# Activation sums for two groups in one instruction, the last group's casts inside an output projection, and one load on ScalarE's queue

## The chip, the cores and the metric

The kernel runs on one core of one Trainium2 chip. A core has a matrix engine (TensorE, "PE" in the profile; its weight loads are "PEld"), three engines for elementwise work (VectorE "DVE", ScalarE "ACT", GpSimd "POOL"), and a sync engine (SyncE, "SP") that here only issues transfers. Each engine has its own instruction queue, which it works off in order; ScalarE's queue can issue transfers as well. The metric is the device time of one execution in microseconds (us). Times in the trace are us from the start of the span.

## What is computed

Block-wise linear attention with a decay for each head (batch 4, 8 heads, 768 positions, head size 64) gives x with 3072 rows of 512; a gated feed-forward block with a hidden size of 1536 follows.

```python
intra = np.einsum('bhic,bhjc->bhij', qb, kb) * Dmask[None]
intra = np.einsum('bhij,bhjd->bhid', intra, vb)
inter = np.einsum('bhid,bhde->bhie', qb * lam_pow[None], kv_state)
out[:, :, sl] = intra + inter
kv_state = lam_block[None, :, None, None] * kv_state + np.einsum('bhsd,bhse->bhde', kb_dec, vb)
...
g = x @ w_gate
silu = g * (1.0 / (1.0 + np.exp(-g)))
val = x @ w_val
return (silu * val @ w_out).astype(np.float32)
```

## The kernel before

**Tiles and groups.** The 3072 rows are six tiles t = 0..5 of 512 rows; each tile is two groups of 256 rows, so there are twelve groups g = 0..11, and tile t needs groups 2t and 2t+1. For a group: k, q and v are loaded (`load_group`, line 263: for the later groups four transfers of 128 KB for k, four for q, two of 256 KB for v, all on SP's queue, L122); k is cast by ScalarE and q is scaled by VectorE (`cast_scaled`, L278 and L280), then one transposing transfer on SP turns both (L271); v is scaled by GpSimd (`v_scale`, L258). `attend(g)` (line 858) issues the inter products of group g (L498), the state update of group g+1 (L404, copied out by ScalarE at L426), the scores of group g+1 (L372, masked by VectorE at L377), the intra products of group g (L511), and two ScalarE copies into the activations `xt` (L523). GpSimd's `state` (L459) adds up states; for groups 8 to 10 ScalarE copies them to bf16 (L439, L441) some steps later, out of a list that `kv_flush` empties.

**Feed-forward, tiles 0 to 3.** A step (`ffn_fc`) takes 128 of the 1536 hidden columns: four gate matmuls (L554) into one PSUM bank, Silu on ScalarE (L558), four value matmuls (L570) into another bank, and VectorE's product of the two into `h` (L573). There are eight banks, used in turn, so a matmul waits until the bank that it writes has been read. Tiles 2 and 3 have twelve steps each; `plan` lists by hand what else is issued after a step's matmuls.

**Sums and differences.** The output projections from tile 1 on (`out_units`), and the hidden layer of tiles 4 and 5 (`ffn_unit`), use seven block products in place of eight. They need sums of operands, all on VectorE: of `wo` (L619), of `h` (`h_combo`, L636), of the weights (`w_combo`, L662) and of the activations (`x_combo`, L679). One call of `x_combo(t, n, g)` is one of four sums for one group of tile t, an instruction over 128x256 elements. So a tile takes eight; sums are read by `ffn_unit` of that tile alone.

**The order around the change.** VectorE's order is written out by hand in two ways. Work in `plan` follows a given step. Work in the list `trickle` is issued from its head, a few at a time (`drip`): one or two after each step whose plan holds no attend, cast or v_scale, and between the products of `out_units`, whose argument `many` (M2 for tile 2, M3 for tile 3) says how many follow each pair of products, and at three places of `ffn_unit` (D0, D1, D2).

In the twelve steps of tile 3 (steps 0 to 11, lines 1109 to 1139): cast of group 10 and load of group 11 after step 6; w_combo after steps 8 and 9; `attend(9)` after step 10; the sums of tile 4's first group after step 8 (line 1139, XC = 8); the cast of group 11 after step 11 (line 1135, C11 = 11). Then: `out_units(2)` (line 1169), seven pairs of products p1, p7, p6, p2, p5, p4, p3, with the second group's sums of tile 4 at the head of `trickle` (line 1168); `ffn_unit(4, 0)`, which holds the scores of group 11 (`early`) and the inter products of group 10; `ffn_unit(4, 1)` with tile 5's first-group sums ahead in `trickle` (line 1193); `out_units(3)` with the second group's (line 1197); `ffn_unit(4, 2)`; and tile 5.

The sums of tile 4 take a buffer of the pool that also holds the transposed q and k (`qkt`, three buffers); those of tile 5 one of the ten `raw` buffers that the loads of k and q use.

Of the kernel before, what the change touches and what calls it, by code (L numbers as in the profile page):

```python
# [19 lines left out]
@with_exitstack  # L20
def kernel(
    ctx: ExitStack,
    tc: tile.TileContext,
    q: bass.AP,
    k: bass.AP,
    v: bass.AP,
    lam: bass.AP,
    moe_w_gate: bass.AP,
    moe_w_val: bass.AP,
    moe_w_out: bass.AP,  # L30
    out: bass.AP,
):
    nc = tc.nc
    with tc.manual_schedule():
        _body(ctx, tc, nc, q, k, v, lam, moe_w_gate, moe_w_val, moe_w_out, out)


def _body(ctx, tc, nc, q, k, v, lam, moe_w_gate, moe_w_val, moe_w_out, out):
# [62 lines left out]
    def gsrc(t, g, h0):  # L101
        b, i = groups[g]
        return bass.AP(tensor=t.tensor,
                       offset=t.offset + b * H * S * D + i * 2 * BLK * D + h0 * S * D,
                       ap=[[2 * D, 2 * M], [S * D, H - h0], [1, 2 * D]])
# [3 lines left out]
    def load_fp32(g, eng, src, what, h0=0, h1=H):  # L109
        if (what, g) not in st:  # L110
            st[(what, g)] = (v_pool if what == "v" else raw_pool).tile(
                [128, H, 2 * D], FP32, name=what, tag="v" if what == "v" else "raw")
        t = st[(what, g)]
        if g < NAT0:
            eng.dma_start(out=t[:, h0:h1], in_=gsrc(src, g, h0)[:, 0:h1 - h0])  # L115
            return
        b, i = groups[g]
        base = src.offset + b * H * S * D + i * 2 * BLK * D
        parts = [(0, 128, False)] if what == "v" else [(0, M, False), (M, M, True)]
        for s in range(2):  # L120
            for p0, n, rev in parts:
                eng.dma_start(  # L122
                    out=t[p0:p0 + n, :, s * D:s * D + D],
                    in_=bass.AP(tensor=src.tensor,
                                offset=base + (H - 1) * S * D * rev + (p0 + s * BLK) * D,
                                ap=[[D, n], [-S * D if rev else S * D, H], [1, D]]))
# [82 lines left out]
    def qfac(g):  # L209
        return bap(dec, [[8, H], [1, 2], [0, D]], 2) if g < NAT0 else bap(qdn, [[2, H], [1, 2], [0, D]])  # L210
# [52 lines left out]
    def load_group(g, parts="kqv"):  # L263
        for src, what in ((k, "kraw"), (q, "qraw"), (v, "v")):
            if what[0] in parts:
                load_fp32(g, nc.sync, src, what)

    def dma_transpose(g):
        t = st[("qk", g)]
        tt = qkt_pool.tile([128, 2, 2, HP, 128], BF16, name="qkt", tag="qkt")  # L270
        nc.sync.dma_start(out=tt.rearrange("p a s h n -> p (a s h) n"),  # L271
                          in_=t.rearrange("p a s x -> p (a s x)"), transpose=True)
        st[("qkt", g)] = tt

    def cast_scaled(g, eng=nc.vector):
        t = qk_pool.tile([128, 2, 2, H * D], BF16, name="qk", tag="qk")
        st[("qk", g)] = t
        nc.scalar.copy(out=t[:, 0].rearrange("p s (h d) -> p h s d", h=H),  # L278
                       in_=st[("kraw", g)].rearrange("p h (s d) -> p h s d", s=2))
        eng.tensor_tensor(out=t[:, 1].rearrange("p s (h d) -> p h s d", h=H),  # L280
                                in0=st[("qraw", g)].rearrange("p h (s d) -> p h s d", s=2),
                                in1=qfac(g), op=ALU.mult)
        dma_transpose(g)
# [35 lines left out]
                        op=ALU.mult)  # L319


    later = []

    def run_later(n):
# [123 lines left out]
    def state(g):  # L448
        b, i = groups[g]
        last = i == NG // B - 1  # L450
        us = st[("ups", g)]
        f = None if i == 0 else kvs[b]
        kv = st.setdefault(("kv", g), [kv0[b][i % 2]])
        for n, u in enumerate(us):
            if f is None:
                f = u
            else:
                o = kv_pool.tile([128, HP, D], FP32, name="kvf", tag="kvf", bufs=4)
                nc.gpsimd.tensor_tensor(out=o, in0=f, in1=u, op=ALU.add)  # L459
                f = o  # L460
            if n == (3 if g >= NAT0 else 1):
                nc.gpsimd.tensor_tensor(out=kvs[b], in0=f, in1=bap(lamgrp, [[1, HP], [0, D]]), op=ALU.mult)
                nc.gpsimd.tensor_copy(out=kv0[b][(i + 1) % 2], in_=kvs[b])
            elif len(kv) == n + 1:
                o = kv_pool.tile([128, HP, D], BF16, name="kvn", tag=f"kvn{n}", bufs=2)
                kv.append(o)
                if g in KVA:
                    kvq.append((len(kvq_now), lambda g=g, n=n, o=o, f=f: kv_copy(g, n, o, f, nc.scalar.copy)))
                else:
                    kv_copy(g, n, o, f, nc.gpsimd.tensor_copy)  # L470
# [47 lines left out]
    def evac(g, fns=(nc.scalar.copy, nc.scalar.copy)):  # L518
        op, xt = st[("op", g)], st[("xt", g // 2)]
        for r in range(2):  # L520
            if fns[r] is None:
                continue
            fns[r](out=xt[:, g % 2, :, r].rearrange("p h (m s) -> p h s m", s=2) if g < NAT0 else  # L523
                   xt[:, g % 2, :, :, r * M:r * M + M],
                   in_=op[r].rearrange("p (h s m) -> p h s m", h=HP, s=2))
# [112 lines left out]
    trickle = []  # L638

    def drip(n):  # L640
        for _ in range(min(n, len(trickle))):
            trickle.pop(0)[1]()
# [25 lines left out]
    def x_combo(t, n, g):  # L668


        xt = st[("xt", t)]
        b11, b12 = xt[:, g, 0:KH, 0], xt[:, g, 0:KH, 1]
        b21, b22 = xt[:, g, KH:MC, 0], xt[:, g, KH:MC, 1]
        if t not in xs:
            pool, tag = (qkt_pool, "qkt") if t == XS0 else (raw_pool, "raw")
            xs[t] = pool.tile([128, 3, 2, KH, BLK], BF16, name="xs", tag=tag)
        x = [xs[t][:, m, g] for m in range(3)]
        o, i0, i1 = ((x[0], b12, b11), (x[1], b22, x[0]), (x[2], b21, x[1]), (b12, b22, b12))[n]
        nc.vector.tensor_tensor(out=o, in0=i0, in1=i1, op=ALU.subtract)  # L679
# [318 lines left out]
    def step(t, fc, b0=0, b1=B):  # L998
        steps.append((t, fc, b0, b1))
        return len(steps) - 1  # L1000

    def at(n, fn, *a):
        plan.setdefault(n, []).append((fn, a))
# [3 lines left out]
    at(s0[2], w_cast)  # L1007
    at(s0[2], w_piece, 8, 10)
    at(s0[3], load_group, 2, "kq")
    at(s0[3], w_piece, 10, 12)  # L1010
    at(s0[3], swapped_q_table)
    at(s0[4], w_cast)
    at(s0[4], state, 1)
    at(s0[4], load_fp32, 2, nc.sync, v, "v", 0, H // 2)
    at(s0[4], load_fp32, 2, nc.sync, v, "v", H // 2, H)
    at(s0[5], load_group, 3)
    at(s0[6], w_cast)
    at(s0[7], load_group, 4, "kq")
    at(s0[7], cast_half, 2, 0, (ACTC, POOLC))
    at(s0[7], cast_half, 2, 1, (ACTC, POOLC))  # L1020
# [6 lines left out]
    at(s0[9], run_later, 4)  # L1027
    at(s0["11a"], upd_core, 2, SPLIT)
    at(s0[10], cast_scaled, 3, nc.gpsimd)
    at(s0[10], load_group, 4, "v")  # L1030
    at(s0["11b"], v_scale, 3, nc.gpsimd)
# [4 lines left out]
    s1a = [step(1, fc, 0, 2) for fc in range(FC)]  # L1036
    s1b = [step(1, fc, 2, 4) for fc in range(FC)]
    at(s1a[3], cast_scaled, 4)
    at(s1a[3], load_group, 5, "v")
    for c in range(0, FC, 2):  # L1040
# [54 lines left out]
    XC = 8  # L1095
    D0 = (0, 0, 3)
    D1 = (0, 0, 3)
    D5 = 0
# [4 lines left out]
    KM = 2  # L1103
    A8 = 5
    A9 = 10
    C11 = 11
    sns = {0: s1a, 1: s1b + s2h}
    AT = {2: (7, 10), 3: (A8, A9)}
    for t in range(2, 4):
        order = [c for j in range(FC // 4) for c in (2 * j, 2 * j + 1, FH + 2 * j, FH + 2 * j + 1)]  # L1110
        sn = [step(t, fc, 2 if t == 2 and fc < NH else 0) for fc in (range(FC) if t == 2 else order)]
# [20 lines left out]
            at(sn[7], h_combo, t, (0, 2))  # L1132
        at(sn[11], h_combo, t, 2)
    sn = sns[3]
    at(sn[C11], cast_scaled, 11)
    for x, n, i, j0, j1 in WS:
        at(sns[x // 100][x % 100], w_combo, i, n, (j0, j1))
    for n in (0, 3, 1, 2):
        at(sn[XC], x_combo, 4, n, 0)

    for n, (t, fc, b0, b1) in enumerate(steps):
        if t >= 1 and t + 1 < NG // 2 and ("xt", t + 1) not in st:
# [19 lines left out]
    def soon(fn, *a):  # L1162
        return 0, lambda: fn(*a)

    def x_soon(t, g):
        return [soon(x_combo, t, n, g) for n in (0, 3, 1, 2)]

    trickle[:0] = x_soon(4, 1)
    out_units(2, many=list(M2))
    for c in range(2):  # L1170
        v_scale(11, nc.gpsimd, c * H // 2, (c + 1) * H // 2)
# [5 lines left out]
    def mid(g):  # L1177
        fixed[:] = [s0, s1]
        core_a(g)
# [10 lines left out]
    upd_copy(11)  # L1190
    intra(10, False)
    state(11)
    trickle[D5:D5] = x_soon(5, 0)
    ffn_unit(4, 1, (aG, aV, eG, eV, bG, bV), lambda: evac(10), lambda: mid(11), D1)
    core_b(11)
    drip(sum(x[0] <= 3 for x in trickle))
    trickle[:0] = x_soon(5, 1)
    out_units(3, bk=(aG, eG, bG, aV, eV, bV), many=list(M3))
    aG, aV, eG, eV, bG, bV, s0, s1 = aG, aV, bG, bV, s0, s1, eG, eV
    ffn_unit(4, 2, (aG, aV, eG, eV, bG, bV), dr=D2)  # L1200
# [41 lines left out]
```

## Time and profile before

| what | value |
|---|---|
| runs of the kernel, median of 3 (lowest to highest) | 221.33 us (220.85 to 221.67) |
| the profiled execution | 221.05 us |
| its span, first to last instruction | 218.9 us |
| TensorE busy, share of the span | 210.0 us, 96% |
| VectorE | 150.8 us, 69% |
| ScalarE | 129.8 us, 59% |
| GpSimd | 93.5 us, 43% |
| mean granted clock of TensorE | 0.997 |

The span leaves out what lies ahead of the first and behind the last instruction, 2.15 us here. An engine's busy time counts its compute instructions only; issuing a transfer and waiting for a semaphore aren't in it. In a timeline a line has the start, the length, the engine and source line, the operation with its output and inputs, how many were merged, and in brackets how long the engine stood idle ahead of it and whose end released it. "SPq" and "ACTq" stand for work of a queue itself, such as issuing a transfer. The chain of waits is the work that ended last, followed back from the last instruction.

### The profile page before, as it was taken

The numbers are of one execution on the slowest core, as the hardware profiler recorded it, in microseconds if no ns is written. First come the engines' busy times: TensorE is split into PE (matmuls) and PEld (weight loads), VectorE is DVE, ScalarE is ACT, GpSimd is POOL, SyncE is SP. The second block draws the span as 40 slices with busy tenths as digits, with TensorE's granted clock in tenths as the row PEclk, the third lists the DMA queues.
The fourth block names the chain that finished last, engine by engine and source line by source line (L and its number), as shares of the span: only waits on it lengthen the run. The fifth ranks groups of instructions, "written<-read, shape, count | busy, mean of one in ns | idle before, by whom it ended". The sixth has DMA issues, their size and how long they took to land.

```text
span 218.9 us, 6889 instructions
## 1 busy us (share of the span) xinstructions
PE 210.0 (96%) x2816; PEld 153.1 (70%) x2816; DVE 150.8 (69%) x275; ACT 129.8 (59%) x280; POOL 93.5 (43%) x126
## 2 busy tenths in 40 slices
PE   8889989999999999999999997999999999999993
PEld 4666435888888447766654544888788888888882
DVE  1764336576687989866387979796798479961750
ACT  6788567656636154638376677655882766636522
POOL 6675645727598150776854236130650022200200
PEclk9999999999999999999999999999999999999998
DMA  6999999999997977989679859782000400004014
GB/s 188 345 350 333 376 339 302 294 238 234 314 366 146 205 209 179 245 200 252 154 175 256 182 128 209 166 202 85 4 4 3 192 0 3 0 3 192 0 51 145
DMA packets 88321, 39.77 MB, mean 182 GB/s; under 512 B 57698, under 2 KB 83938, under 8 KB 88290
## 3 DMA queue, kind: packets, MB, share of 16 engines
q1 hardware_dynamic: 87090, 38.74, 65.5%
q10 hardware_dynamic: 1200, 0.59, 0.9%
q8 instruction: 22, 0.36, 0.7%
q14 instruction: 9, 0.07, 0.1%
HBM read 28.31 MB, written 6.29 MB: 158 GB/s over the span
## 4 chain that ended last, share of the span: by engine, by line
PE 78%; DMA 8%; SPq 6%; DVE 2%; ACT 1%; issue 1%; POOL 1%; POOLq 1%; DVEq 0%
PE bank L788 21%; PE bank L570 16%; PE bank L554 16%; PE bank L698 15%; PE bank L589 5%; DMA qraw<-in_q_dram 4%; DMA wraw<-in_moe_w_val_dram 3%; SPq L115 3%; SPq L233 3%; PE bank L511 2%; PE bank L498 2%; PE bank L404 1%; PE bank L346 1%; ACT sil L725 1%; PE bank L372 1%
## 5 line engine op out<-in xcount | busy, mean ns | idle before, releaser
L573 DVE TENSOR_TENSOR h<-sil,bank 128x256 bf16<-128x256 bf16 (+1 forms) x67 | 34.9, 532 | 27.1 <-PE bank L570 17.3
L570 PE MATMUL bank<-xt,wv_sb 128*128 128x256 bf16 (+1 forms) x268 | 52.4, 319 | 0.7 <-DVE h L573 0.7
L554 PE MATMUL bank<-xt,wg_sb 128*128 128x256 bf16 (+1 forms) x268 | 52.5, 319 | 0.0
L558 ACT ACTIVATE sil<-bank 128x256 bf16<-128x256 f32 (+1 forms) x67 | 31.8, 479 | 23.2 <-PE bank L554 18.5
L570 PEld LDWEIGHTS <-wv_sb 128*128 128x128 bf16 x268 | 26.1, 98 | 16.5 <-issue 1.0
L258 POOL TENSOR_TENSOR v_s<-v,dec 128x512 bf16<-128x512 f32 (+1 forms) x18 | 24.3, 1364 | 25.1 <-DMA v<-in_v_dram 16.5
L554 PEld LDWEIGHTS <-wg_sb 128*128 128x128 bf16 x268 | 25.2, 98 | 13.7 <-DVE xt L523 0.2
L728 POOL TENSOR_TENSOR h<-sil,es 128x512 bf16<-128x512 bf16 x6 | 7.0, 1163 | 49.3 <-ACT sil L725 49.3
L788 PEld LDWEIGHTS <-h 128*128 128x128 bf16 x240 | 23.3, 98 | 3.5 <-issue 0.3
L788 PE MATMUL bank<-wo_sb,h 128*128 128x256 bf16 x180 | 21.6, 273 | 0.1
L788 PEld LDWEIGHTS <-hs 128*128 128x128 bf16 x180 | 17.6, 98 | 2.9
L353 DVE TENSOR_TENSOR ssb<-bank,causal 128x512 bf16<-128x512 f32 x24 | 15.4, 682 | 1.8 <-PE bank L346 1.8
L698 PEld LDWEIGHTS <-ws 128*128 128x128 bf16 x144 | 13.8, 97 | 2.4 <-issue 0.2
L459 POOL TENSOR_TENSOR kvf<-kvs,ups 128x256 f32<-128x256 f32 x8 | 6.7, 839 | 19.8 <-ACT ups L426 19.8
L740 DVE TENSOR_TENSOR bank<-bank,es 128x512 f32<-128x512 f32 x12 | 7.8, 693 | 10.5 <-PE bank L698 9.0
L788 PE MATMUL bank<-wt,hs 128*128 128x256 bf16 x120 | 15.0, 272 | 0.0
L725 ACT ACTIVATE sil<-bank 128x512 bf16<-128x512 f32 x18 | 10.7, 594 | 6.9 <-POOL h L728 4.6
L728 DVE TENSOR_TENSOR h<-sil,bank 128x512 bf16<-128x512 bf16 x18 | 12.3, 683 | 1.5 <-ACT sil L725 1.4
L523 ACT CAST xt<-bank 128x512 bf16<-128x512 f32 x19 | 11.6, 655 | 2.4 <-PE bank L511 1.9
L698 PE MATMUL bank<-xs,ws 128*128 128x256 bf16 x96 | 13.0, 272 | 0.0
L459 POOL TENSOR_TENSOR kvf<-kvf,ups 128x256 f32<-128x256 f32 x16 | 12.6, 785 | 0.9
L698 PE MATMUL bank<-xt,wg_sb 128*128 128x256 bf16 x72 | 10.8, 273 | 0.2 <-ACT ups L426 0.2
(119 smaller groups left out, 362.9 us busy)
## 6 DMA issues: line engine op xcount, KB each, us to landing
out_dram<-osb SPq DMA_DIRECT2D x22, 256.0 KB, 2.1
v<-in_v_dram SPq DMA_DIRECT2D x18, 256.0 KB, 4.6
woraw<-in_moe_w_out_dram SPq DMA_DIRECT2D x6, 512.0 KB, 7.3
kraw<-in_k_dram SPq DMA_DIRECT2D x24, 128.0 KB, 3.2
qraw<-in_q_dram SPq DMA_DIRECT2D x24, 128.0 KB, 3.3
wraw<-in_moe_w_gate_dram SPq DMA_DIRECT2D x5, 512.0 KB, 7.7
wraw<-in_moe_w_val_dram SPq DMA_DIRECT2D x5, 512.0 KB, 6.6
kraw<-in_k_dram SPq DMA_DIRECT2D x4, 512.0 KB, 6.6
```

Source lines behind the costliest of these rows:

```text
L258: eng.tensor_tensor(out=st[("vs", g)][:, h0:h1], in0=st[("v", g)][:, h0:h1].rearrange("p h (s d) -> p h s d", s=2), in1=vfac(g, h0, h1), o ...
L353: nc.vector.tensor_tensor(out=ssb[:, h2, 2 * c:2 * c + 2].rearrange("p a s n -> p a (s n)"), in0=sp[(c, h2)].rearrange("p (a x) -> p a x", ...
L459: nc.gpsimd.tensor_tensor(out=o, in0=f, in1=u, op=ALU.add)
L523: fns[r](out=xt[:, g % 2, :, r].rearrange("p h (m s) -> p h s m", s=2) if g < NAT0 else xt[:, g % 2, :, :, r * M:r * M + M], in_=op[r].rea ...
L554: nc.tensor.matmul(gp[:, 0:N], wg_sb[:, mc, fs], xt[:, b0 // 2:b1 // 2, mc].rearrange("p g b n -> p g (b n)"), start=(mc == 0), stop=(mc = ...
L558: nc.scalar.activation(sil[:, 0:N], gp[:, 0:N], AF.Silu)
L570: nc.tensor.matmul(vp[:, 0:N], wv_sb[:, mc, fs], xt[:, b0 // 2:b1 // 2, mc].rearrange("p g b n -> p g (b n)"), start=(mc == 0), stop=(mc = ...
L573: nc.vector.tensor_tensor(out=h_sb[:, fc % FH, b0:b1].rearrange("p b n -> p (b n)"), in0=sil[:, 0:N], in1=vp[:, 0:N], op=ALU.mult)
L698: nc.tensor.matmul(o[:, fi * 256:fi * 256 + 256], lhs(i, c, 2 * j + fi), rhs(c), start=(start and fi == 0 and c == 0), stop=(c == KH - 1), ...
L725: nc.scalar.activation(sil[key], src, AF.Silu)
L728: eng.tensor_tensor(out=h_of(half, r), in0=v3(sil[half, r]), in1=v3(src), op=ALU.mult)
L788: nc.tensor.matmul(o, lhs(f), rhs(f), start=(start and f == 0), stop=(f == FH - 1), skip_group_check=True)
```

## The change

1. `x_combo` takes None for the group: one instruction then covers both groups (128x512 elements). Tiles 4 and 5 use it (XM = (1, 1)): four sums each, not eight. The four of tile 4 after step 8 of tile 3 and the four of tile 5 ahead of `ffn_unit(4, 1)` are gone; the joined sums are issued inside `out_units(2)` and `out_units(3)`.
2. The cast of group 11 (ScalarE copy, VectorE product, transposing transfer on SP) goes from the plan of step 11 into `trickle`: its order in `out_units(2)` is "cxwh", the cast, the four sums, nothing for w (W3L is empty), then what was in the list. With M2 beginning 1, 1, 0, 2, 1 the cast follows p1, the first sum p7, two sums p2, the last p5. Step 11's plan then has no cast, so it drips.
3. The four transfers of k of group 11 are issued by ScalarE's queue (KACT), behind the cast of group 10 and ahead of step 7's Silu; those of q and v stay on SP's.

QP is empty, so the line in `cast_scaled` changes nothing.

```diff
     def load_group(g, parts="kqv"):
         for src, what in ((k, "kraw"), (q, "qraw"), (v, "v")):
             if what[0] in parts:
-                load_fp32(g, nc.sync, src, what)
+                load_fp32(g, nc.scalar if what == "kraw" and g in KACT else nc.sync, src, what)
...
+    QP = ()
+
     def cast_scaled(g, eng=nc.vector):
+        eng = nc.gpsimd if g in QP else eng
...
+    KACT = (11,)
...
         xt = st[("xt", t)]
+        g = slice(0, 2) if g is None else slice(g, g + 1)
         b11, b12 = xt[:, g, 0:KH, 0], xt[:, g, 0:KH, 1]
...
-    C11 = 11
+    C11 = None
...
-    at(sn[C11], cast_scaled, 11)
+    if C11 is not None:
+        at(sn[C11], cast_scaled, 11)
+    XM = (1, 1)
+    W3L = ()
+    TR2 = "cxwh"
...
-    for n in (0, 3, 1, 2):
-        at(sn[XC], x_combo, 4, n, 0)
+    if not XM[0]:
+        for n in (0, 3, 1, 2):
+            at(sn[XC], x_combo, 4, n, 0)
...
-    trickle[:0] = x_soon(4, 1)
+    xw = dict(x=x_soon(4, None if XM[0] else 1),
+              c=[soon(cast_scaled, 11)] if C11 is None else [],
+              w=[soon(w_combo, i, 3, (j, j + 1)) for j in W3L for i in range(2)], h=trickle[:])
+    trickle[:] = [y for z in TR2 for y in xw[z]]
+    trickle += [] if "h" in TR2 else xw["h"]
+    trickle += [] if "c" in TR2 else xw["c"]
     out_units(2, many=list(M2))
...
-    trickle[D5:D5] = x_soon(5, 0)
+    trickle[D5:D5] = [] if XM[1] else x_soon(5, 0)
     ffn_unit(4, 1, (aG, aV, eG, eV, bG, bV), lambda: evac(10), lambda: mid(11), D1)
     core_b(11)
     drip(sum(x[0] <= 3 for x in trickle))
-    trickle[:0] = x_soon(5, 1)
+    trickle[:0] = x_soon(5, None if XM[1] else 1)
     out_units(3, bk=(aG, eG, bG, aV, eV, bV), many=list(M3))
```

## The prediction

> **What bounds the kernel now.** I read the page's chain of waits first, then the chain in order of time, then the engines' timelines around its non-TensorE pieces, then where transfers land. All times are us from the span's start; the span is 218.9.
>
> The chain by line, from the page:
>
> ```profile
> PE 78%; DMA 8%; SPq 6%; DVE 2%; ACT 1%; issue 1%; POOL 1%; POOLq 1%; DVEq 0%
> ```
>
> The DMA and SPq shares lie in the first 31.7 us, which the change doesn't touch. From there on the end is set by TensorE, so an edit is worth what it takes from, or adds to, TensorE's idle time. The chain in order of time (start, length, what) leaves TensorE only a few times in the half that is touched; the first place is this:
>
> ```profile
> 133.16 0.42 PE bank L498 x32
> 133.64 0.56 issue
> 134.21 0.42 DVE h L636
> 134.62 0.34 DVE hs L636
> 134.96 1.13 DVE wv_sb L662
> 136.09 0.61 DVE h L573
> 136.74 1.02 PE bank L570 x4
> 137.76 9.17 PE bank L788 x84
> ```
>
> VectorE is what TensorE waits for at the last step of tile 3. TensorE's timeline there (start, length, idle before) has the two holes:
>
> ```profile
> 134.34 0.44 PE L372 MATMUL bank<-qkt 64*64 64x64 bf16 x30 [0.53 <-DVE h L573]
> ...
> 134.99 1.04 PE L554 MATMUL bank<-xt,wg_sb 128*128 128x512 bf16 x4
> 136.74 1.02 PE L570 MATMUL bank<-xt,wv_sb 128*128 128x512 bf16 x4 [0.71 <-DVE h L573]
> 137.60 2.78 PE L788 MATMUL bank<-wo_sb,h 128*128 128x256 bf16 x24
> ```
>
> 0.53 + 0.71 = 1.24 us idle: a score and a value product wait for PSUM banks that VectorE's L573 products free. After 137.60 TensorE runs without a hole to 146.9, and then shows one of 0.18 us at 155.85. VectorE's own timeline says why it is late:
>
> ```profile
> 130.75 1.03 DVE L662 TENSOR_TENSOR wg_sb<-wg_sb 128x1024 bf16<-128x1024 bf16 x1
> 131.70 1.13 DVE L679 TENSOR_TENSOR xs<-xt 128x256 bf16<-128x256 bf16 x1
> 132.87 0.29 DVE L679 TENSOR_TENSOR xt<-xt 128x256 bf16<-128x256 bf16 x1
> 133.08 0.61 DVE L679 TENSOR_TENSOR xs<-xt,xs 128x256 bf16<-128x256 bf16 x2
> 133.61 0.68 DVE L573 TENSOR_TENSOR h<-sil,bank 128x512 bf16<-128x512 bf16 x1
> ```
>
> The four activation sums (L679) for tile 4's first group stand in front of step 9's product, whose matmuls ended near 131.4. They hold VectorE from 131.70 to 133.61, 1.9 us.
>
> **Part 1: the sums of tile 4 leave step 8.** Without them step 9's product runs at 131.78, when the L662 before it ends; two L636 of step 9 (pitch 0.33 each) end by 133.1; the second L662 (1.03 to 1.21) ends by 134.1 to 134.3; step 10's product (0.6) ends by 134.9. The scores want their bank at 133.62: freed at 132.4, so 0.53 us goes. The last value product would start 0.53 + 0.71 earlier than 136.74, at 135.50: bank freed at 134.9, so 0.71 us goes too, with 0.6 us to spare. Both holes: -1.24. Behind it the output projection of tile 2 starts at 136.36; its fourth bank needs the mask L377, which follows step 10's product and ends near 135.5. Its last needs the other mask, behind step 11's product: 137.7, wanted near 138.4.
>
> **Part 2: where the sums go.** Four of 512 elements instead of eight of 256. The trace has none of this size at L679; the 512-element L636 takes 0.42, pitch 0.34 (165.8 to 171). So 1.4 us replaces 1.9 and 1.9 (before, the second four spanned 141.61 to 144.25, less L813's 0.76). They stand in the projection, where VectorE has room, and the first reader is the product after 147. Cost nothing; without cover 1.4 us. Nearest deadline: p6's sums L813 free the bank that p4 reads at 142.9 in the shifted projection. VectorE before it: step 11's product to 137.1, mask 137.7, one L636 of 512 and one of 1024 (they move forward, since step 11 no longer counts as busy) to 138.7, group 11's cast 1.22 to 139.9, one sum to 140.3, then L813 to 141.1. Margin 1.8 us. Bounds: one sum at 0.42, or at the worst L679 seen, 1.13; no loss either way. The Trainium skill, "SBUF — State Buffer", section on the shared port pair, speaks against this place: a VectorE instruction with two SBUF inputs and a GpSimd instruction reading SBUF exclude each other, and v_scale of group 11 will run here. The trace agrees in kind (1.13 against 0.29 for the same sum, v_scale running from 130.19). If the rule held VectorE for both halves of v_scale (2.2 us), L813 would end at 143.3 and the estimate by that page would be -0.8 instead of -1.24.
>
> Tile 5 moves in the same way from the second unit of tile 4 into its own projection, before 165.8. TensorE shows no wait in either place (162.22 to 171.40 is back to back): nothing, against 1.4 us uncovered.
>
> **Part 3: the casts of group 11 after the first products.** One ScalarE copy (1.05), one VectorE product (1.22), one transposing DMA on SP. They move one product pair later in the program, but VectorE stood waiting for q before (0.97 us idle at 140.13, released by the q transfer). With k gone from SP's queue, q is issued from 131.48, not 134.20, and lands near 137.5 to 138. The transpose then issues near 140.0 instead of 141.49; landing after 4.1 (141.49 to 145.59) gives 144.1; the scores of group 11 read it at 147.4. Cover 3.3 us; nothing. ScalarE's copy lands between its projection copies with 0.3 us of room. v of group 11 also comes 2.7 us earlier; its reader is far off.
>
> **Part 4: four k transfers on ScalarE's queue.** They stand behind the cast of group 10 and in front of step 7's Silu:
>
> ```profile
> 126.11 1.04 ACT L278 CAST qk<-kraw 128x1024 bf16<-128x1024 f32 x1
> 127.16 0.60 ACT L558 ACTIVATE sil<-bank 128x512 bf16<-128x512 f32 x1
> 128.88 0.60 ACT L558 ACTIVATE sil<-bank 128x512 bf16<-128x512 f32 x1 [1.13 <-PE bank L554]
> 129.50 0.83 ACT L439 CAST kvn<-kvf 64x256 bf16<-64x256 f32 x2
> ```
>
> SP's row for the same transfers:
>
> ```profile
> 131.48 2.67 SPq L122 DMA_DIRECT2D kraw<-in_k_dram  x4
> ```
>
> Price of one: ScalarE's own two (0.43 and 0.53, another shape) and SP's median for k, 0.633. Four: 1.7 to 2.5; with one at SP's longest, 1.36, 3.3. No row shows whether the first can issue under the cast (from 126.15) or only behind it (127.15). ScalarE is then free for step 7 between 127.85 and 130.4. Behind it wait two Silus, the state copies (L439, L441), a Silu and the last state copies: packed as the trace packs them 0.6 + 3.23 = 3.83 us. The first TensorE reader is the inter product of group 9 (L498) at 133.09. So ScalarE may be free as late as 129.26 for nothing; every us beyond that is one of TensorE. I take SP's 0.633 and the early start, 128.7: no cost. With the late start 129.7: 0.45. At the end of the range 130.4: 1.15. A loss below zero is excluded: the queue only gains work. The buffer isn't waited for: k of group 11 follows k of group 9, cast at 113.99.
>
> A rule of the Trainium skill speaks against this part: "DMA: Bandwidth & Descriptors", section on issuing engines, says that a second issuing engine saves only sequencer time, since all transfers run on the same 16 engines. The rows bear on that so: v of group 10 is in flight (landed 130.03), and its v_scale starts at 130.19 and feeds the update at 133.37. If k's 512 KB went wholly ahead of the 297 KB moved after 127.5, at 290 GB/s v would land 0.8 later and TensorE lose about 0.15. With fair shares it lands as before, since the engines stood at 0.23 and 0.45 busy in half-us stretches there. I take zero. The estimate by the page would be -1.1.
>
> **Sum.** -0.53 - 0.71 + 0 + 0 = -1.24 on the profiled execution (221.05, which is its span and 2.15 around it): 219.8. The median of the runs, 221.33, lies 0.28 above that execution, so 220.1.
>
> **Rivals.**
> - *ScalarE's queue takes part of it back* (end product late): late start plus ordinary issues, 0.45, or one long issue, 1.15, leaves a gain of 0.8 to 0.1. For: the 1 us of slack ahead of L498 is all there is. Against: the idle 1.13 before step 8's Silu absorbs most. 220.8.
> - *Slower: issues at ScalarE's queue block like SP's slow ones.* SP's second v of group 10 took 2.09 (125.15 to 127.24), the longest k 1.36. If a limit shared by the queues makes each of the four 1.36 from 126.15, ScalarE is free at 131.6, the state copies end at 135.4, L498 is 2.3 late: +1.1, 222.4. It decides from 130.5 on, an average issue of 0.84 to 1.1. Against: of 24 k issues the median is 0.633.
> - *The sums do no harm where they are:* VectorE's lateness is only replaced by another wait at the same place (Silu of step 10, ups copies before the projection). The projection's first bank needs the ups copies at 134.82, the Silu ends near 133.4: against. 221.2.
>
> **How the numbers follow.** The forecast (both holes closed, cost up to 0.2) 0.56; the first rival 0.20; no change 0.08; slower 0.16. Runs of one kernel here differ by 0.8 (220.85 to 221.67), so a step under 0.5%, 1.1 us, isn't told from none. The forecast's 220.1 lies just past that bound (220.22), so of its 0.56 some 0.08 falls within; a gain a little above the sum is in the rest. Faster 0.50, same 0.33, slower 0.17. The range: down to 219.4, if the 0.18 hole at 155.85 closes too and the median falls half the spread low; up to 221.6, through the first rival and no change. The likeliest case's own range is 219.5 to 220.5.
>
> **What would show it.** Right: no idle time above 0.1 us in front of L372 and the last L570 of tile 3; L679 eight times at 128x512; step 9's product near 131.8; the output projection near 136.4. Part 4 right: four issues on ScalarE's queue near 126.2 to 128.7 and the state copies done before 133. Wrong: idle before L498 near 133 released by L439; issues above 0.8 us; a v_scale of group 10 that starts after 131; L813 released late enough that p4 waits. If the holes close and the time doesn't fall by about as much, a new hole stands behind 137.

## The result, and the profile after

| | before | after |
|---|---|---|
| runs, median of 6 each on the same chip (lowest to highest) | 221.19 us (219.30 to 221.68) | 218.31 us (217.54 to 219.23) |
| ratio to before, 95% interval | | 0.989 [0.9856, 0.9923] |
| the profiled execution / its span | 221.05 / 218.88 us | 218.10 / 216.29 us |

The changed kernel is faster, by more than was forecast: 2.9 us by the medians, 1.7 to 3.2 by the interval, where 1.1 to 1.2 had been predicted (220.1 for the median). The measured 218.31 lies below the range (219.4 to 221.6). New line numbers are 3 to 5 higher: products L577, scores L376, sums of the activations L684, of `h` L640, of the weights L666, projection L793.

The two holes are gone. In the chain of waits in order of time (start, length, what), the four pieces of VectorE between the score products and the last value product no longer occur:

```profile
132.63 0.38 PE bank L502 x32
133.01 0.19 PE bank L408 x19
...
133.26 0.34 PE bank L376 x27
133.59 0.32 PE bank L515 x32
133.91 0.97 PE bank L558 x4
134.88 0.86 PE bank L574 x4
135.75 9.17 PE bank L793 x84
```

TensorE's timeline has no bracket (idle time) there, ahead of neither the scores nor the last value products:

```profile
132.56 0.21 PE L502 MATMUL bank<-qkt,kv 64*64 64x64 bf16 x1
...
133.07 0.53 PE L376 MATMUL bank<-qkt 64*64 64x64 bf16 x29
133.43 0.49 PE L515 MATMUL bank<-ssb,v_s 64*64 64x64 bf16 x32
133.84 1.04 PE L558 MATMUL bank<-xt,wg_sb 128*128 128x512 bf16 x4
134.72 1.03 PE L574 MATMUL bank<-xt,wv_sb 128*128 128x512 bf16 x4
135.58 2.78 PE L793 MATMUL bank<-wo_sb,h 128*128 128x256 bf16 x24
```

From the first inter-group product of group 9 to the projection of tile 2 TensorE needs 135.58 - 132.56 = 3.02 us; before, it was 137.60 - 133.09 = 4.51. I call this **the stretch**.

VectorE's timeline shows why: step 9's product (131.01) follows the weight sum L666 with no activation sum between.

```profile
129.93 0.68 DVE L666 TENSOR_TENSOR wg_sb<-wg_sb 128x1024 bf16<-128x1024 bf16 x1
131.01 0.69 DVE L577 TENSOR_TENSOR h<-sil,bank 128x512 bf16<-128x512 bf16 x1 [0.40 <-ACT sil L562]
131.62 1.19 DVE L640 TENSOR_TENSOR h<-h 128x512 bf16<-128x512 bf16 x1
132.73 0.41 DVE L640 TENSOR_TENSOR hs<-hs,h 128x512 bf16<-128x512 bf16 x1
133.06 0.68 DVE L666 TENSOR_TENSOR wv_sb<-wv_sb 128x1024 bf16<-128x1024 bf16 x1
133.67 0.67 DVE L577 TENSOR_TENSOR h<-sil,bank 128x512 bf16<-128x512 bf16 x1
```

ScalarE's timeline with the transfers that its queue issues (ACTq):

```profile
125.15 0.69 ACTq L122 DMA_DIRECT2D kraw<-in_k_dram  x1
125.65 1.05 ACT L281 CAST qk<-kraw 128x1024 bf16<-128x1024 f32 x1
125.87 2.12 ACTq L122 DMA_DIRECT2D kraw<-in_k_dram  x3
128.09 1.08 ACT L562 ACTIVATE sil<-bank 128x512 bf16<-128x512 f32 x2 [1.40 <-PE bank L574]
129.20 0.83 ACT L443 CAST kvn<-kvf 64x256 bf16<-64x256 f32 x2
```

Four issues, one about every 0.70 (0.60 to 0.69 each). They stand behind the cast in ScalarE's list, but the first began 0.50 ahead of the cast's start. They end at 127.99, and the Silu behind them, which waited for TensorE, starts at 128.09. Nothing behind them is late.

The last difference lies at the span's end. ScalarE issues the last output transfer here, before and after:

```profile
215.52 0.37 ACTq L794 DMA_DIRECT2D out_dram<-osb  x1
```

```profile
213.40 0.37 ACTq L799 DMA_DIRECT2D out_dram<-osb  x1
```

From there to the end of the span it is 218.88 - 215.52 = 3.36 us before and 216.29 - 213.40 = 2.89 after. Up to this row the two kernels run the same instructions for the last 45 us. I call this **the end**.

So the difference of the two profiled executions, 221.05 - 218.10 = 2.95, is made up as follows: stretch 1.49; end 0.48; what lies outside the span 0.36 (2.17 to 1.81); 0.10 between the projection's start and the last matmul; and 0.53 ahead of the stretch (its start moved from 133.09 to 132.56). The last isn't of the change: an early inter-group product (L498 before, L502 after) that waits for ScalarE starts at 39.74 before and at 38.72 after, so the kernel before was 1.02 late long ahead of the first transfer that differs (125.15).

### The profile page after: what moved, and what is told of

Same layout as the page of the kernel before. It is cut to its first block, busy times and chain, and to the rows that moved or that the text cites. A ratio compares the mean times of both kernels' runs of the same rounds, so it can differ in the third digit from the quotient of the medians.

```text
span 216.3 us, 6883 instructions
## 1 busy us (share of the span) xinstructions
PE 209.8 (97%) x2813; PEld 153.3 (71%) x2816; DVE 149.5 (69%) x267; ACT 129.1 (60%) x280; POOL 92.3 (43%) x126
## 3 DMA queue, kind: packets, MB, share of 16 engines
q10 hardware_dynamic: 3312, 1.11, 2.0%
## 4 chain that ended last, share of the span: by engine, by line
PE 73%; DVE 7%; DMA 6%; SPq 5%; ACT 3%; issue 2%; POOL 2%; POOLq 1%; DVEq 0%
PE bank L793 20%; PE bank L703 15%; PE bank L558 13%; PE bank L574 13%; DMA woraw<-in_moe_w_out_dram 4%; PE bank L593 4%; SPq L122 2%; DMA qraw<-in_q_dram 2%; SPq L247 2%; DVE ws L666 2%; DVE h L577 1%; PE bank L515 1%; PE bank L146 1%; DVE wt L623 1%; PE bank L502 1%
## 5 line engine op out<-in xcount | busy, mean ns | idle before, releaser
L577 DVE TENSOR_TENSOR h<-sil,bank 128x256 bf16<-128x256 bf16 (+1 forms) x67 | 34.8, 531 | 26.3 <-PE bank L574 18.0
L793 PEld LDWEIGHTS <-h 128*128 128x128 bf16 x240 | 23.3, 98 | 3.4 <-issue 0.3
L793 PE MATMUL bank<-wo_sb,h 128*128 128x256 bf16 x180 | 21.6, 273 | 0.1
L793 PEld LDWEIGHTS <-hs 128*128 128x128 bf16 x180 | 17.6, 98 | 2.9
L793 PE MATMUL bank<-wt,hs 128*128 128x256 bf16 x120 | 15.0, 272 | 0.0
```

Of the source, the lines that this page charges most:

```text
L577: nc.vector.tensor_tensor(out=h_sb[:, fc % FH, b0:b1].rearrange("p b n -> p (b n)"), in0=sil[:, 0:N], in1=vp[:, 0:N], op=ALU.mult)
L793: nc.tensor.matmul(o, lhs(f), rhs(f), start=(start and f == 0), stop=(f == FH - 1), skip_group_check=True)
```

## The experiments

Fifteen runs on four chips, each timed beside the kernel before on the same chip. For each kernel: the ratio; from its profile the stretch and the end; "around", its median of execution time less span; and the numbers of instructions in SP's and VectorE's lists, counted in the compiled program. (The expectations measure the end from the last matmul's start, which adds 0.60.)

| kernel | ratio [95%] | stretch | end | around | SP / VectorE |
|---|---|---|---|---|---|
| before | | 4.51 | 3.36 | 2.12 | 214 / 442 |
| after | 0.989 [0.9856, 0.9923] | 3.02 | 2.89 | 1.78 | 210 / 438 |
| r1 before again | 1.0003 [0.9965, 1.0041] | 4.35 | 3.36 | 2.11 | 214 / 442 |
| r2 after again | 0.991 [0.9878, 0.9942] | 3.03 | 2.88 | 1.75 | 210 / 438 |
| e1 sums only | 0.997 [0.9928, 1.0012] | 3.22 | 3.35 | 1.72 | 214 / 434 |
| e2 cast only | 0.9977 [0.9936, 1.0017] | 6.03 | 3.36 | 1.93 | 214 / 446 |
| e3 k only | 1.0009 [0.9976, 1.0042] | 6.25 | 2.88 | 2.08 | 210 / 442 |
| e4 tile 4's sums back | 1.0015 [0.997, 1.0059] | 3.80 | 2.88 | 2.11 | 210 / 442 |
| e5 k back | 0.9955 [0.9919, 0.9991] | 3.04 | 3.35 | 1.73 | 214 / 438 |
| e6 cast back | 0.9899 [0.9864, 0.9934] | 3.10 | 2.87 | 1.75 | 210 / 435 |
| e7 before + k of group 10 | 0.9964 [0.9928, 1.0] | 3.28 | 2.87 | 2.10 | 210 / 442 |
| e8 before, sums after step 11 | 1.0201 [1.0157, 1.0245] | 3.02 | 3.35 | 2.16 | 214 / 442 |
| e9 moved, not joined | 0.9934 [0.9902, 0.9966] | 3.75 | 2.88 | 1.95 | 210 / 440 |
| e10 k of groups 10 and 11, cast back | 0.9977 [0.9936, 1.0018] | 3.05 | 2.88 | 1.89 | 206 / 435 |
| e11 four more on SP | 0.9922 [0.9889, 0.9956] | 3.19 | 3.34 | 1.75 | 214 / 438 |
| e12 four more on VectorE | 0.9903 [0.9866, 0.994] | 3.67 | 2.89 | 2.08 | 210 / 442 |
| e13 after + k of group 10 | 0.9902 [0.9868, 0.9936] | 3.05 | 2.87 | 1.95 | 206 / 436 |

A stretch is that of one execution; executions of one kernel differ by 1 to 3 us, so the ratios tell what a part is worth and the profiles tell by what. One profile needn't be a usual execution: e4's (219.15) is the fastest of its twelve, whose median is 221.07, and in e5's the granted clock was at half for 3.4 us early on (0.992 in the mean).

### One part alone, and one part undone

e1 (sums moved and joined, nothing else), against the changed kernel:

```diff
-    KACT = (11,)
+    KACT = ()
-    C11 = None
+    C11 = 11
```

> Only the sums are joined and moved; the cast of group 11 stays after step 11 and k of group 11 stays on SP's queue. Theory (VectorE held by the four sums after step 8 opens both holes at group 9's attend): no hole in front of the scores or the last value product of tile 3, 1.5 us gained between the inter products of group 9 and the output projection of tile 2 (4.51 before, 3.02 after the change), the run 1.5 us shorter, some 219.7. Rival (the casts or the k loads carry the gain, since VectorE stands at group 11's cast waiting for q): holes stay, gain below 0.3. Where the span differs ahead of 124 us it is told by the two landmarks alone: inter products of group 9, start of the projection.

e2 (the cast alone):

```diff
-    KACT = (11,)
+    KACT = ()
-    XM = (1, 1)
+    XM = (0, 0)
```

> Only the cast of group 11 moves into the projection; sums in their old places and sizes, k on SP's queue. Theory: both holes stay (0.53 and 0.71 idle, 4.5 us from the inter products of group 9 to the projection), the time within 0.4 of the kernel before. Rival (cast carries the gain): 1 us or more gained in that stretch.

e3 (k on ScalarE's queue alone): `C11 = 11`, `XM = (0, 0)`.

> Only k of group 11 on ScalarE's queue; sums and cast as before. Theory: both holes stay, 4.5 us in the stretch, time within 0.4 of the kernel before; the four issues take 2.1 to 2.8 us on ScalarE's queue and lie under the cast of group 10. Rival 1 (it carries the gain): 1 us or more gained. Rival 2 (it costs TensorE something that the rest of the change hides): slower than before by 0.3 to 1.0.

e4 (all of the change but the sums of tile 4): `XM = (0, 1)`.

> The whole change, but tile 4's sums go back: eight of 256 elements, the first four after step 8. Theory: both holes return, 4.5 us in the stretch, and 1.5 us of the change's gain is lost: some 219.8 where the change has 218.3. Rival (the gain of 2.9 is made somewhere else, ahead of 124 us or behind the last matmul, by the other parts): the time stays near 218.3.

No part alone brings the gain, and with tile 4's sums back at step 8 (e4) all of it is gone: 1.0015, though the end stays 0.48 shorter. (e4's profile doesn't show the loss: its stretch is 3.80, and its one hole there is another, told of below.) The stretch is short wherever the sums are away from step 8 (e1, 3.22), and it isn't a fixed 4.51 where they are there. e3 has 6.25. Its VectorE timeline (brackets: idle time and whose end released it):

```profile
128.59 1.23 DVE L283 TENSOR_TENSOR qk<-qraw,qdn 128x1024 bf16<-128x1024 f32 x1 [0.96 <-DMA qraw<-in_q_dram]
...
131.63 1.14 DVE L684 TENSOR_TENSOR xs<-xt 128x256 bf16<-128x256 bf16 x1
132.80 1.02 DVE L684 TENSOR_TENSOR xt<-xt 128x256 bf16<-128x256 bf16 x1
133.75 0.60 DVE L684 TENSOR_TENSOR xs<-xt,xs 128x256 bf16<-128x256 bf16 x2
134.27 0.68 DVE L577 TENSOR_TENSOR h<-sil,bank 128x512 bf16<-128x512 bf16 x1
...
136.60 1.21 DVE L666 TENSOR_TENSOR wv_sb<-wv_sb 128x1024 bf16<-128x1024 bf16 x1
137.73 0.68 DVE L577 TENSOR_TENSOR h<-sil,bank 128x512 bf16<-128x512 bf16 x1
```

and the holes on TensorE that follow from it:

```profile
135.00 0.44 PE L376 MATMUL bank<-qkt 64*64 64x64 bf16 x30 [0.70 <-DVE h L577]
...
138.46 1.02 PE L574 MATMUL bank<-xt,wv_sb 128*128 128x512 bf16 x4 [1.78 <-DVE h L577]
```

VectorE waits 0.96 us for q, and its cast of group 10 starts only 4.48 us ahead of the stretch (5.07 in the changed kernel). But q isn't all of it. Two of the four sums take 1.14 and 1.02 in place of 0.29, while GpSimd runs v_scale of group 10 beside them:

```profile
131.42 2.25 POOL L258 TENSOR_TENSOR v_s<-v,dec 128x512 bf16<-128x512 f32 x2 [4.67 <-PE bank L574]
```

Before, it was one sum of 1.13, under this v_scale:

```profile
130.19 2.50 POOL L258 TENSOR_TENSOR v_s<-v,dec 128x512 bf16<-128x512 f32 x2 [3.46 <-DMA v<-in_v_dram]
```

So what the sums cost depends on what GpSimd runs at the same time. The second hole seems to grow in the same way: the weight sum L666 at 136.60 takes 1.21 (0.68 in the changed kernel) beside GpSimd's state additions. The table has the six kernels with the sums at step 8, ordered by when step 9's product starts (us from the start of the stretch; a minus is ahead of it; the sums are counted from the first one's start to that product).

| kernel | cast of group 10 | first sum starts | four sums take | step 9's product | stretch |
|---|---|---|---|---|---|
| e7 | -5.53 | -1.24 | 1.06 | -0.18 | 3.28 |
| e4 | -4.82 | -1.79 | 1.79 | 0.00 | 3.80 (0.53 of it the other hole) |
| r1 | -4.85 | -1.56 | 1.91 | 0.35 | 4.35 |
| before | -4.68 | -1.39 | 1.91 | 0.52 | 4.51 |
| e2 | -4.08 | -0.79 | 1.90 | 1.11 | 6.03 (0.31 of it a wait for the transposed q) |
| e3 | -4.48 | -1.44 | 2.64 | 1.20 | 6.25 |

The stretch follows step 9's product in all six. It doesn't follow the cast, and so the lateness of q, by itself: e4 has the cast of r1 and no hole of VectorE's, e3 has an earlier cast than e2 and a longer stretch. A late first sum (e2) or slow sums (e3) make the product late.

### The stretch by another way: q and v of group 10 earlier

e7 leaves the sums at step 8 and takes k of group 10, not 11, from SP's queue, so that q and v of group 10 are issued sooner. Against the changed kernel:

```diff
-    KACT = (11,)
+    KACT = (10,)
-    C11 = None
+    C11 = 11
-    XM = (1, 1)
+    XM = (0, 0)
```

> The kernel before with one thing changed: the four transfers of k of group 10, not 11, on ScalarE's queue. Tile 4's first sums stay after step 8. Theory A (the hole follows q of group 10): SP issues that q 2.7 us earlier, VectorE's cast starts 1 us or more earlier against the inter products of group 9 (5.3 or more), and the stretch to the projection falls from 4.4 to under 3.9. The end is 3.48 with 210 instructions on SP's queue as with k of group 11. Rival (the sums' place alone sets the hole): 4.4 again, end 3.48, time 0.5 under the kernel before.

VectorE's timeline of e7:

```profile
126.99 1.22 DVE L283 TENSOR_TENSOR qk<-qraw,qdn 128x1024 bf16<-128x1024 f32 x1
...
131.28 0.28 DVE L684 TENSOR_TENSOR xs<-xt 128x256 bf16<-128x256 bf16 x1
...
132.34 0.68 DVE L577 TENSOR_TENSOR h<-sil,bank 128x512 bf16<-128x512 bf16 x1
```

The cast doesn't wait for q, step 9's product runs at 132.34 (e3: 134.27; before: 133.61) with all four sums ahead of it, and TensorE has no hole: stretch 3.28. But the sums don't start sooner against the stretch than before (1.24 ahead of it, before 1.39). They take 1.06 instead of 1.91, since v_scale, whose v came earlier too, is over at 130.82, ahead of the first sum:

```profile
128.76 2.06 POOL L258 TENSOR_TENSOR v_s<-v,dec 128x512 bf16<-128x512 f32 x2 [2.56 <-DMA v<-in_v_dram]
```

So the holes were VectorE's backlog at step 9's product, made of the four sums that stood there and of the time that they lost beside GpSimd; e7 takes the second part away from the sums, and the change takes the sums away. How much of it an earlier q alone would take away isn't shown, since no run moved q without v. The whole gained less than this one profile says (0.9964, interval up to 1.0); its median span, 217.0, is 0.5 above that of its profiled execution.

### Where the sums may go

e8 is the kernel before with the four sums behind the cast of group 11 instead of after step 8:

```diff
-    XC = 8
+    XC = 11
```

> The kernel before with one constant changed: the four sums of tile 4's first group after step 11, not step 8; nothing joined, cast and k as before. Theory (what stands ahead of step 9's and step 10's products is all that matters for the holes): stretch 3.0 to 3.3, both holes gone. VectorE then waits for q of group 11 ahead of the sums, or behind them; a new wait of up to 0.5 in the projection is possible, as in the run with the sums alone. End 3.96, 2.1 around the span (442 instructions in VectorE's list, 214 in SP's). Time 1.0 to 1.5 under the kernel before. Rival: the holes need the joining or the move into the projection, and stay.

The stretch is 3.02, and yet it is the slowest of all, 1.0201. VectorE waits for q of group 11 (k stands ahead of it on SP's queue), and everything behind the cast waits along: the sums of tile 4 and one of `h` (the last three of these take 1.34 and 1.26 beside v_scale of group 11, without it 0.61 and 0.42), and behind them the sums L813 of the projection. VectorE's row, then TensorE's:

```profile
139.10 1.23 DVE L280 TENSOR_TENSOR qk<-qraw,qdn 128x1024 bf16<-128x1024 f32 x1 [2.57 <-DMA qraw<-in_q_dram]
```

```profile
144.22 1.62 PE L788 MATMUL bank<-wt,hs 128*128 128x256 bf16 x12 [3.55 <-DVE bank L813]
```

From the projection's start to the last matmul e8 takes 83.00 us, before 77.31. That is 5.7 more, and the hole is 3.55 of it. Much of the rest is the clock: the page's row of the granted clock (40 slices of 5.5 us, in tenths) falls once in mid-run, right behind the hole.

```profile
PEclk9999999999999999999999999969999999999998
```

From 145.4 to 148.8 it was 0.50. 3.4 us at half speed cost TensorE some 1.7 us, an estimate. All six runs of e8 have a mean clock of 0.989 to 0.992; the others have so low a clock in at most three of their runs. That the hole brings the clock down is likely from this, but no run here tries it by itself.

e1 has the same wait in small: 1.33 us for q at 138.81, and a hole:

```profile
141.57 1.47 PE L793 MATMUL bank<-wt,hs 128*128 128x256 bf16 x12 [0.24 <-DVE bank L818]
```

In e5 (cast moved, k still on SP), e6 (k on ScalarE, cast not moved) and the changed kernel this hole is absent: either of the two parts covered it there. e10 below shows that k on ScalarE's queue doesn't always do so.

e5, k back on SP's queue: `KACT = ()`.

> The whole change, but k of group 11 goes back to SP's queue (sums and cast moved). Theory: the stretch stays at 3.0 to 3.3; the cast of group 11 waits for q as before, up to 1.5 us, in the projection, with nothing of TensorE behind it; the end is 3.96 and not 3.48, if that half us belongs to SP's shorter queue. So some 0.5 slower than the changed kernel. Rival: k on ScalarE's queue is worth nothing or costs: same or faster.

e6, the cast back after step 11: `C11 = 11`.

> The whole change, but the cast of group 11 goes back behind step 11 (sums moved, k on ScalarE's queue). Theory: stretch 3.0 to 3.3, end 3.48, time within 0.3 of the changed kernel: with k and q early the cast has nothing to wait for in either place. Rival: in its old place it keeps step 11 from dripping and VectorE's later sums late, TensorE waits in the projection: 0.5 or more slower.

Beside them the two kernels again, unchanged:

> The kernel before, unchanged, for a second profile. Theory A (the hole at group 9's attend is not of one size: it grows with the lateness of q of group 10, since the four sums and what follows then meet GpSimd's v_scale and state additions): the stretch from the inter products of group 9 to the projection of tile 2 lies between 4.0 and 6.3 us and follows the time from VectorE's cast of q of group 10 to those inter products, longer where that is under 4.7. Theory B (a hole of fixed size): 4.5 again, whatever that time is.

> The changed kernel again. Theory A and B: the stretch is 3.0 to 3.3 us whenever q of group 10 lands, since nothing that can wait stands ahead of step 9's product; time 1 to 1.5% under the kernel before. The end, from the last matmul's start to the end of the span, 3.48 as in all runs with four issues fewer on SP's queue, against 3.96.

Moving the cast is worth nothing in this pair, with k on ScalarE's queue in both (0.9899 against 0.991). Moving k is worth 0.0045 of the time by the two ratios, about 1.0 us, with intervals that overlap; 0.48 of it is the end.

e9 moves the sums of tile 4 but leaves them eight:

```diff
-    M2 = (1, 1, 0, 2, 1, 2, 2)
+    M2 = (1, 2, 0, 4, 2, 2, 2)
-    xw = dict(x=x_soon(4, None if XM[0] else 1),
+    xw = dict(x=x_soon(4, 0) + x_soon(4, 1),
```

> The whole change, but tile 4's sums are eight of 256 elements in the projection (the counts of the list are raised so that all are issued there). Theory (joining is worth nothing to TensorE): stretch 3.0 to 3.3, no hole in the projection over 0.3, time within 0.3 of the changed kernel. Rival (VectorE has no room there for eight): a hole of 0.4 or more in front of p4's products, time 0.4 or more above. What lies around the span, 1.7 or 2.1, tells whether it follows VectorE's list: 440 instructions here, between 438 (1.75) and 442 (2.1).

0.9934: most of the gain is the move. There is no hole in its projection either. Its stretch of 3.75 has another one, of 0.64, which is the next point.

### What k on ScalarE's queue does to v

e9's TensorE waits in the state update, for v of group 10; so do e4 (0.53) and e12 (0.56). e12's rows, TensorE first, then GpSimd:

```profile
133.24 0.29 PE L410 MATMUL bank<-v_s,qk 64*64 64x64 bf16 x11 [0.56 <-POOL v_s L260]
```

```profile
130.96 2.24 POOL L260 TENSOR_TENSOR v_s<-v,dec 128x512 bf16<-128x512 f32 x2 [5.10 <-DMA v<-in_v_dram]
```

v_scale of group 10 starts 1.2 us ahead of the stretch there (e4 1.18, e9 1.20). In the six profiles in which k of group 11 stays on SP's queue and k of group 10 too (before, r1, e1, e2, e5, e8) it starts 2.3 to 3.3 ahead. In the eight with only k of group 11 on ScalarE's, it is 1.2 to 3.7, and three of the eight have the hole. So k's transfers, running beside those of v, seem to make v late in some executions; that it is they and nothing else wasn't tried by itself. With k of group 10 there too, v is issued earlier, and the start is 3.4 to 3.8 ahead (e7, e10, e13).

e10 and e13 try this as a better version. e10: `KACT = (10, 11)`, `C11 = 11`.

> The sums as changed, the cast of group 11 back behind step 11, and k of groups 10 and 11 on ScalarE's queue: a try at something better. VectorE's cast of group 10 then doesn't wait for q. Theory: TensorE has no hole left there, so stretch 3.0 to 3.1 again and time within 0.3 of the changed kernel; 206 instructions on SP's queue leave the end at 3.48. Rival: four more issues on ScalarE's queue behind group 9's cast make its Silus late, a hole of 0.3 or more ahead of group 8's attend, and the time rises.

e13: `KACT = (10, 11)` alone.

> The changed kernel with k of group 10 too on ScalarE's queue, so that q of group 10 lands earlier as well. Theory (q of group 10 was what step 8's end waited for, and the sums already take that wait away): stretch 3.02 to 3.1, end 3.48, no hole in the projection, so no gain over the changed kernel: a ratio of 0.990 to 0.993. Rival (the earlier q and v are worth something further down): 0.987 or less.

e10 is worse than the changed kernel (0.9977), with a hole in the projection. Its cast doesn't wait for q. With the cast out of the list, two joined sums instead of one stand ahead of L818, and both meet v_scale of group 11:

```profile
138.11 2.27 POOL L258 TENSOR_TENSOR v_s<-v,dec 128x512 bf16<-128x512 f32 x2 [2.04 <-PE bank L793]
```

```profile
138.20 1.27 DVE L684 TENSOR_TENSOR xs<-xt 128x512 bf16<-128x512 bf16 x1
139.50 1.15 DVE L684 TENSOR_TENSOR xt<-xt 128x512 bf16<-128x512 bf16 x1
140.58 0.75 DVE L818 TENSOR_TENSOR bank<-bank,osb 128x256 f32<-128x256 f32 x2
```

```profile
141.05 1.47 PE L793 MATMUL bank<-wt,hs 128*128 128x256 bf16 x12 [0.39 <-DVE bank L818]
```

e13 has no hole and is no better than it either (0.9902). No version tried beats the changed kernel beyond the uncertainty.

### The end, and what lies around the span

In the table the end is 3.34 to 3.36 in the seven kernels with 214 instructions on SP's list and 2.87 to 2.89 in the ten with 210 or 206, whatever else is changed. "Around" is 2.08 to 2.16 wherever VectorE's list has 442. The last two tests put four instructions back and nothing else. e11, behind the first unit of tile 4 (issued from 146.37; they don't stand after step 5, as the expectation has it), into a tile that nothing reads:

```diff
+    for n in range(4):
+        nc.sync.dma_start(out=pad[0:1, 8 * n:8 * n + 8], in_=bass.AP(tensor=lam.tensor, ...))
```

> The changed kernel with four tiny transfers more on SP's queue (the 21 lam values into a tile that nothing reads, after step 5), so that SP's list has as many instructions as before the change (214 instead of 210) while k of group 11 stays on ScalarE's queue. Theory A (the end after the last matmul follows the length of SP's list): the end goes back from 3.48 to 3.96, the stretch from the inter-group products of group 9 to the projection stays at 3.02 to 3.1, and the whole is about 0.5 above the changed kernel, a ratio near 0.993. Rival (the end was shortened by where k is loaded, whatever the number of instructions): the end stays at 3.48 and the ratio stays at 0.990 to 0.991.

e12, at the start:

```diff
+    for n in range(4):
+        nc.vector.memset(pad[0:1, n:n + 1], 0.0)
```

> The changed kernel with four one-element memsets more on VectorE, at the start, into a tile that nothing reads: VectorE's list has 442 instructions as before the change instead of 438. Theory A (what lies around the span follows the length of VectorE's list): execution time less span goes back from 1.75 to about 2.1, the end stays at 3.48, the stretch at 3.02 to 3.1, and the whole is about 0.35 above the changed kernel, a ratio near 0.993. Rival (the time around the span has another cause): it stays at 1.75, and the ratio at 0.990 to 0.991.

Both answers are plain. e11's last row of ScalarE's queue, its span being 217.38:

```profile
214.04 0.37 ACTq L799 DMA_DIRECT2D out_dram<-osb  x1
```

217.38 - 214.04 = 3.34: the end is back, with k still on ScalarE's queue. Around stays at 1.75. In e12 around is back at 2.08 while the end stays at 2.89. Single records show the pause of the end on SP: from its last wait for an output transfer to its next instruction it is 0.37 us before (217.61 to 217.98), 0.38 in e11, 0.04 after. Why a list of 214 pauses there and one of 210 doesn't is open. One row of the pages goes along: of the DMA queue q14, which carries instructions, it counts 9 packets in the span in six of the seven kernels with 214, and 8 in the ten others and in e2, where the ninth starts 0.02 us behind the span's end. Before and after:

```profile
q14 instruction: 9, 0.07, 0.1%
```

```profile
q14 instruction: 8, 0.07, 0.1%
```

It is a load of instructions that starts about 0.25 us ahead of the span's end in the six, and 0.6 to 1.6 behind it in the ten; whether it has to do with the pause isn't shown. The rule for around is open too: 446 on VectorE's list gave 1.93, 440 gave 1.95, and 435 and 436 with five more on ScalarE's gave 1.89 and 1.95, so it doesn't simply grow with one list. By the ratios, neither 0.47 nor 0.33 us can be told from nothing (0.9922 and 0.9903 against 0.989 and 0.991); both are shown by the spans and the times around them, not by the whole.

## Why the prediction was right or wrong

**Where it failed: the sum.** The prediction wrote "-0.53 - 0.71 + 0 + 0 = -1.24 on the profiled execution (221.05, which is its span and 2.15 around it)". It carried over as fixed what lies behind the last matmul and around the span. Both fell, by 0.48 and 0.34, since the change takes four transfers from SP's list and four instructions from VectorE's; e11 and e12 each give one of them back and leave the other. These two terms, 0.82 together, were missing. No row of the one profile that it had shows them.

**Part 1, the holes: right in mechanism, a little small.** The holes closed, and e1 and e8, with k and the cast as before, show that moving the sums does it alone; e4's ratio says the same the other way round. They were worth 1.49 in the first pair of profiles and 4.35 - 3.03 = 1.32 in the second, where 1.24 was forecast. The brackets count idle time from the modelled end of a matmul, while by starts the two holes of before were 0.62 and 0.87, which is 1.49. Taking them as of a fixed size was also too simple: with the sums at step 8 the stretch lay between 3.28 and 6.25 in other profiles, by when the sums started and whether v_scale met them. The prediction saw that meeting (1.13 against 0.29 for the same sum) but used it only against the new place.

**The rest of the 2.95** is the 0.53 ahead of the stretch, an accident of the two executions: the changed kernel's own second profile starts its stretch at 132.36, e11's, with the same work ahead of it, at 133.02. Without it, 1.3 to 1.5 + 0.48 + 0.34 gives 2.1 to 2.3. The two ratios, 0.991 and 0.989, are 2.0 (1.3 to 2.7) and 2.4 (1.7 to 3.2) us.

**Part 2, where the sums go: no cost, but not by the margin that it gave.** The joined sums took 1.27, 0.60, 0.41 and 0.41; the first runs under v_scale of group 11 (138.88 to 141.30). L818 ended at 141.07 (forecast 141.1), and TensorE didn't wait. The "margin 1.8 us" was a misreading: it took p4 for the first that waits for L818. In the kernel p5 writes the bank that L818 reads, and p5 comes before p4. The projection also began 0.78 sooner than forecast (135.58, not 136.36), while L818 came at the forecast time.

```profile
139.13 1.27 DVE L684 TENSOR_TENSOR xs<-xt 128x512 bf16<-128x512 bf16 x1
140.32 0.75 DVE L818 TENSOR_TENSOR bank<-bank,osb 128x256 f32<-128x256 f32 x2
```

```profile
140.82 1.47 PE L793 MATMUL bank<-wt,hs 128*128 128x256 bf16 x12
```

The first of the two L818 ends at 140.74, and p5 starts at 140.82. In e1 and e10, where p5 does wait, it starts 0.05 behind that end, so some 0.03 us was left: luck more than forecast. The Trainium skill ("SBUF — State Buffer", section on the shared port pair) agrees in kind, 1.27 against 0.41. Here one sum stood ahead of L818 and met only the first half of v_scale, and the -0.8 worked out from that page didn't come. In e10, with two sums there, VectorE was held through both halves, and the hole of 0.39 is about the 0.4 that this estimate took off.

**Part 3, "nothing": right.** The transposing transfer was issued at 139.35 (forecast near 140.0), and the cast didn't wait for q, issued sooner because k has left SP's queue. TensorE has no hole in the projection in e5 either, where the moved cast still waits 0.38 for q with k on SP's queue. e1 (0.24) shows the price with neither part.

**Part 4, no cost on ScalarE: right there, too low elsewhere.** Issues of 0.70 (taken: 0.633), the early start, the state copies in time; the first rival and the slower one fell. But the bound for a late v, "about 0.15", was too small: 0.53 to 0.64 in three executions. The Trainium skill ("DMA: Bandwidth & Descriptors", section on issuing engines) says that a second issuing engine saves only issue time. The late v fits it, and the shorter end is a saving of another kind.

**No change, 221.2** (the sums do no harm where they are) fell with the result and with e4, 1.0015 with the sums back at step 8.

## What to carry to other kernels

When a step's wait is traced to an engine's backlog, ask both what stands in its list ahead of the late instruction and what another engine runs beside it: here moving the four sums closed the holes, and so did leaving them and letting GpSimd's v_scale end before they began. Before work is put behind an instruction that waits for a transfer, list what else is queued behind that instruction: the same four sums were worth 1.3 to 1.5 us in one place and made the kernel about 4.5 slower in another, the lower clock included. For the deadline of a bank, look for the first instruction that writes it again, not only for the one that reads the result: here that left almost no room where 1.8 us had been counted. An edit that changes how many instructions an engine's list holds can move the span's end and what lies around it by some tenths of a us, which no wait in the profile shows; compare these two times before a small difference is put down to the work.

## What was not expected of the hardware

- Four instructions fewer on SP's list shorten the end from 3.36 to 2.89 us, and four tiny transfers put back restore 3.34; a tile that nothing reads is enough.
- Four one-element memsets on VectorE, at the start, lengthen what lies around the span from 1.75 to 2.08 us.
- An issue on ScalarE's queue began before the cast that stands ahead of it in the list: 125.15, the cast 125.65. Issuing four transfers (2.8 us) thus held ScalarE's compute up by nothing.
